# Attention feeding a gated MLP: scores and values head by head, without zero blocks, from the third batch on

## The chip, the cores and the metric

One core of one Trainium2 chip. The time is device microseconds of one execution, the median of three runs. A core has five engines that run side by side: TensorE (PE, matrix products, weights loaded by a queue of its own shown as PEld), VectorE (DVE), ScalarE (ACT), GpSimd (POOL) and SyncE (SP, which here issues every DMA). Each works through its own instructions in order and waits on semaphores for the others.

## The reference

Eight batches of eight heads, 576 queries of 64 dimensions. Keys and values are averaged over groups of 8 positions, so there are 72 of each. The attention result, 4608 tokens of 512 numbers, goes through a gated MLP with 1536 hidden units.

```python
k_p = k.reshape(B, H, Sp, pool, D).mean(axis=3)
v_p = v.reshape(B, H, Sp, pool, D).mean(axis=3)
scores = scale * np.matmul(q, k_p.transpose(0, 1, 3, 2))
attn = np.exp(scores - np.max(scores, axis=-1, keepdims=True))
attn = attn / (np.sum(attn, axis=-1, keepdims=True) + 1e-09)
x = np.matmul(attn, v_p)            # then tokens x (8 heads * 64)
g = x @ w_gate
out = (g / (1 + np.exp(-g)) * (x @ w_val)) @ w_out
```

## The kernel before

Tokens are cut into nine tiles of 512. A tile passes through the MLP in 12 steps of 128 hidden units (`moe`): 24 gate and value matmuls (`side`, lines 591 to 593, every product as high x high, low x high and high x low in 16-bit numbers), then tanh and products on ACT and DVE, then 12 projection matmuls of the step before (`project`, lines 616 to 621). Batches have 576 queries, so tile borders fall inside batches; each tile's attention is done in chunks of at most 128 queries of one batch (`_plan`). From the third batch on there are 24 chunks of 128 queries and 6 of 64.

`x` is what the MLP reads: 512 features on 4 blocks of 128 rows, tokens along the columns, a high part `xh` and a low part `xl`.

The first two batches go through `first_tile`, which interleaves attention, weight loading and the first tile's MLP by the table ORDER: a letter names a job, a number its step. There Lw loads weights, a to n split them; Ls, Lx, Ku, Vr load and sum k and v of the third batch. Everything after it is two generators: the MLP of tile i yields 12 times, and after each step three steps of the attention of tile i+1 are taken (`take(att, 3)`); a scheduler then sets the order on each engine from these by its own time model.

The attention of a chunk from the third batch on (`chunk`): q is scaled and split in a high and a low part (`split_q`, ACT and POOL). `scores` takes two heads at once: the stationary side is q of two heads on 128 rows, the moving side is 144 columns, the 72 keys of each head with zeros in the other head's 64 rows (`kst_h`, `kst_l`); three matmuls for each of four pairs. Softmax follows on DVE and ACT. `soft_high` and `soft_low` write high and low parts of the 72 weights into `half`, 64 positions of each head in 8 blocks and the remaining 8 positions of four heads in 2 more; one DMA transpose on SP turns these 10 blocks (`turned`, line 473) into `pt`. `values` then has V stationary, two heads in one 128x128 block with zeros off the diagonal, and `pt` moving, four matmuls for each of four pairs; the result has features on rows, and ACT and DVE write it straight into `xh` and `xl` (lines 490 and 494).

`prep` prepares a batch: k and v are loaded in pieces into a pool of three buffers (`mid`, which also holds q for its maximum, and the output on its way out), summed on POOL (`pool8`), the largest q, k and v are found on DVE, summed over rows by a matmul with ones (`over_rows`, line 155), and powers of two from these scale the splits.

## Time and profile before

| what | number |
|---|---|
| median of 3 runs | 1008.49 us (1005.98 to 1009.74) |
| profiled execution | 1008.23 us, span 1005.7 us |
| PE busy | 941.1 us, 94% of the span |
| DVE, ACT, POOL busy | 568.0, 411.3, 259.6 us |
| mean granted PE clock | 0.992 |
| DMA | 79.49 MB, 40 transposes of `half`, each 10 blocks |

The span runs from the first to the last instruction of the core, and the time of an execution is 2.5 us longer. Busy times of PE are modelled at their end and overlap, so the distance between the starts of two matmuls tells what one costs in a full PE.

### The profile page before, as it was taken

Reading aid. Unit: us, or ns where it says so; the run is one execution under the profiler, and the core shown is the slowest. Engines: PE = TensorE matmul, PEld = TensorE weight load, DVE = VectorE, ACT = ScalarE, POOL = GpSimd, SP = SyncE. Lnnn points to the kernel's source line nnn. Section 1 sums busy time; section 2 is a strip of 40 time slices with the busy share of each in tenths; the row PEclk is TensorE's granted clock in tenths of the full one; section 3 lists DMA queues with packets and bytes.
Section 4 is the critical chain, followed back from the end, with each engine's and each line's share of the span. In section 5 each row is a group of like instructions: output and inputs, shape, how many; then the busy total and the mean of one; then the engine's idle time right before and its main releaser. Section 6 shows DMA issues by size and latency. Waiting matters only on the chain.

```text
span 1005.7 us, 13356 instructions
## 1 busy us (share of the span) xinstructions
PE 941.1 (94%) x5200; PEld 498.2 (50%) x5200; DVE 568.0 (56%) x1047; ACT 411.3 (41%) x716; POOL 259.6 (26%) x286
## 2 busy tenths in 40 slices
PE   1478888999999999999999999999999999999997
PEld 1366443454545555555455554555455455544443
DVE  9988998467556645664357544735454245323222
ACT  4488886225323432352235423522444244322222
POOL 6656567342106210620061105200111011000000
PEclk9989999999999999999999999999999999999999
DMA  9565752432115200620061206200311011001001
GB/s 353 110 197 159 209 190 77 157 120 43 37 55 173 55 18 32 202 51 6 31 198 42 31 1 217 59 14 6 79 26 33 1 56 27 14 1 42 1 1 42
DMA packets 82942, 79.49 MB, mean 79 GB/s; under 512 B 53696, under 2 KB 70080, under 8 KB 81344
## 3 DMA queue, kind: packets, MB, share of 16 engines
q1 hardware_dynamic: 82880, 78.66, 27.0%
q8 instruction: 40, 0.66, 0.3%
q14 instruction: 22, 0.18, 0.1%
HBM read 57.41 MB, written 9.44 MB: 66 GB/s over the span
## 4 chain that ended last, share of the span: by engine, by line
PE 79%; DVE 14%; DMA 3%; ACT 2%; issue 1%; POOL 1%; SPq 0%; DVEq 0%; ACTq 0%; POOLq 0%
PE gv L591 16%; PE gv L592 16%; PE gv L593 16%; PE acc L616 9%; PE acc L620 8%; PE acc L621 8%; DVE wf L198 2%; DVE wgv_l L230 2%; DVE ws L178 1%; ACT ws L188 1%; PE ps L417 1%; DVE ws L186 1%; DMA k<-k_rows 1%; DVE sm L440 1%; DVE sc L429 1%
## 5 line engine op out<-in xcount | busy, mean ns | idle before, releaser
L591 PE MATMUL gv<-xh,wgv_h 128*128 128x512 f16 (+1 forms) x888 | 331.8, 374 | 12.0 <-DVE hf L602 9.5
L593 PE MATMUL gv<-xh,wgv_l 128*128 128x512 f16 (+1 forms) x888 | 332.0, 374 | 5.3 <-DVE wgv_l L230 5.3
L592 PE MATMUL gv<-xl,wgv_h 128*128 128x512 f16 (+1 forms) x888 | 331.9, 374 | 0.6 <-DVE xl L494 0.6
L602 DVE SCALAR_TENSOR_TENSOR hf<-hf,gv 128x512 f32<-128x512 f32 (+1 forms) x111 | 74.4, 670 | 191.7 <-ACT hf L599 191.6
L620 PE MATMUL acc<-hl,wo_b 128*128 128x512 bf16 (+1 forms) x444 | 167.4, 379 | 1.3 <-POOL hl L744 1.3
L621 PE MATMUL acc<-hb,wo_l 128*128 128x512 bf16 (+1 forms) x444 | 166.5, 377 | 0.0
L616 PE MATMUL acc<-hh,wo_h 128*128 128x512 f32 (+1 forms) x444 | 141.4, 437 | 0.0
L599 ACT ACTIVATE hf<-gv,un 128x512 f32<-128x512 f32 (+1 forms) x111 | 74.8, 674 | 162.5 <-PE gv L593 158.8
L640 ACT CAST hh<-hf 128x512 fp32r<-128x512 f32 x96 | 59.2, 617 | 198.6 <-DVE hf L607 198.4
L593 PEld LDWEIGHTS <-wgv_l 128*128 128x128 f16 x888 | 87.0, 98 | 106.4 <-DVE wgv_l L230 7.8
L592 PEld LDWEIGHTS <-wgv_h 128*128 128x128 f16 x888 | 86.9, 98 | 102.7 <-issue 13.6
L591 PEld LDWEIGHTS <-wgv_h 128*128 128x128 f16 x888 | 88.0, 99 | 91.4 <-ACT wgv_h L225 1.0
L607 DVE SCALAR_TENSOR_TENSOR hf<-gv,un,hf 128x512 f32<-128x512 f32 (+1 forms) x111 | 81.4, 733 | 80.8 <-PE gv L593 79.9
L399 POOL TENSOR_TENSOR ql<-qt,qh 128x512 f16<-128x512 f32 (+1 forms) x30 | 31.9, 1063 | 366.4 <-PE ps L419 231.5
L642 DVE TENSOR_TENSOR hl<-hf,hh 128x512 bf16<-128x512 f32 x96 | 71.8, 748 | 52.2 <-ACT hh L640 52.1
L616 PEld LDWEIGHTS acc<-hh,wo_h 128*128 128x128 f32 x444 | 82.2, 190 | 23.6
L468 POOL TENSOR_TENSOR half<-sc,half 128x512 f16<-128x512 f32 (+1 forms) x40 | 48.4, 1211 | 138.9 <-issue 81.2
L620 PEld LDWEIGHTS <-wo_b 128*128 128x128 bf16 x444 | 43.5, 98 | 65.7 <-issue 28.5
L621 PEld LDWEIGHTS <-wo_l 128*128 128x128 bf16 x444 | 44.1, 99 | 39.4 <-issue 2.2
L641 ACT CAST hb<-hf 128x512 bf16<-128x512 f32 x96 | 58.9, 613 | 0.0
L397 ACT ACTIVATE qt<-qt,inv 128x512 f32<-128x512 f32 (+1 forms) x30 | 20.1, 677 | 66.7 <-DMA qt<-q_rows 58.3
L428 DVE TENSOR_REDUCE mx<-ps 128x4 f32<-128x288 f32 (+1 forms) x80 | 35.7, 449 | 18.4 <-PE ps L419 18.2
(109 smaller groups left out, 1114.9 us busy)
## 6 DMA issues: line engine op xcount, KB each, us to landing
ws<-w_all SPq DMA_DIRECT2D x12, 1536.0 KB, 7.2
out_t<-ob SPq DMA_DIRECT2D x36, 256.0 KB, 2.3
qt<-q_rows SPq DMA_DIRECT2D x32, 256.0 KB, 3.3
vr<-v_main SPq DMA_DIRECT2D x16, 512.0 KB, 5.5
kr<-k_rows SPq DMA_DIRECT2D x14, 576.0 KB, 4.8
qr<-q_rows SPq DMA_DIRECT2D x12, 576.0 KB, 4.9
vr<-v_left SPq DMA_DIRECT2D x8, 512.0 KB, 4.3
k<-k_rows SPq DMA_DIRECT2D x2, 576.0 KB, 8.5
```

Source lines behind the costliest of these rows:

```text
L591: nc.tensor.matmul(o, wh, x["h"][:, j, a:e], start=(j == 0), stop=False)
L592: nc.tensor.matmul(o, wh, x["l"][:, j, a:e], start=False, stop=False)
L593: nc.tensor.matmul(o, wl, x["h"][:, j, a:e], start=False, stop=(j == NJ - 1))
L599: nc.scalar.activation(hf, gate, AF.Tanh, scale=un[:, c, 0:1])
L602: nc.vector.scalar_tensor_tensor(out=hf, in0=hf, scalar=1.0, in1=gate, op0=ALU.add, op1=ALU.mult)
L607: nc.vector.scalar_tensor_tensor(out=hf, in0=val, scalar=un[:, c, 2:3], in1=hf, op0=ALU.mult, op1=ALU.mult)
L616: nc.tensor.matmul(o, wo_h[:, c, js], hh[:, :n], start=begin, stop=False)
L620: nc.tensor.matmul(o, wo_b[:, c, js], hl[:, :n], start=False, stop=False)
L621: nc.tensor.matmul(o, wo_l[:, c, js], hb[:, :n], start=False, stop=end)
L640: nc.scalar.copy(hh[:, :n], hf[:, :n])
L641: nc.scalar.copy(hb[:, :n], hf[:, :n])
L642: nc.vector.tensor_sub(hl[:, :n], hf[:, :n], hh[:, :n].bitcast(F32))
```

## The change

For batches 2 to 7 attention no longer works on two heads at once. A chunk's q comes twice, once on rows 0 to 63 and once on rows 64 to 127, from an array that holds it so (`q_twice`, 8 heads side by side, twice the bytes); `split_q` writes the high part into the upper half of the rows on ACT, and high and then low into the lower half (ACT, DVE). A score product of one head is then two matmuls of 72 columns: against `ka`, the keys' high part on both halves, and `kb`, the low part above zeros.

Softmax weights are laid out as 16 blocks, two a head: 64 high and 64 low, and a block with the 72 high ones, 8 low ones and 8 high ones of the remainder (104 rows). They are turned by one DMA transpose and are now the stationary side; the moving side is 64 columns of `va` or `vb`. The result has queries on rows. ACT and DVE write its high and low part into `xt`, and a second DMA transpose of 8 blocks writes them into `x`, now one tile with both parts.

k and v of a batch come in four pieces each, k with its rows twice, v as 104 rows. All operands of two chunks live in `box`, which takes the two buffers of the weight loads once these are done. The loads and sums of the third batch leave ORDER and are made by the generator during the second tile, as for the other batches. In the generator a chunk's softmax now comes ahead of the values of the chunk before, and two steps more are left ahead of the last values of a tile.

```diff
--- before.py
+++ after.py
+VROWS = 104
...
-d10 P8 w11 d11 x11 V12 e10 y11 T8 Z6 t12 l11 u12 Lx0 n11 f10 e11 O11 g10 m11 v12 h10
+V12 e10 y11 T8 Z6 t12 l11 u12 n11 f10 e11 O11 g10 m11 v12 h10 un10 x12 i10 n10 l10 f11
...
-    halves = [const.tile([P, (2 * NJ + 2) * P], F16, name=f"half{i}") for i in range(2)]
+    halves = [const.tile([P, 2 * H * P], F16, name=f"half{i}") for i in range(2)]
...
+    home = {}
+    turn = [0]
+
+    def box(b):
+
+        if not home:
+            for i in range(2):
+                whole = raw.tile([P, 12 * P * 2], F32, name="box", tag="raw")
+                at16, part = whole.bitcast(F16), {}
+                lo = 0
+                for name, n in (("ka", SP), ("kb", SP), ("va", D), ("vb", D), ("qs", P), ("xt", P)):
+                    part[name] = at16[:, lo : lo + H * n].rearrange("p (h n) -> p h n", h=H)
+                    lo += H * n
+                home[i] = part
+                n = (SP, D)[i]
+                home[("ks", "vs")[i]] = whole[:, lo // 2 : lo // 2 + H * n].rearrange(
+                    "p (h n) -> p h n", h=H
+                )
+                nc.gpsimd.memset(part["kb"][D:], 0.0)
+                nc.gpsimd.memset(halves[i][:, OLD:], 0.0)
+        return home[b % 2]
...
     def prep_k(b):
-        for g in range(2):
-            if ("k", b, g) not in state:
-                k_load(b, g)
-                k_sum(b, g)
-                yield
+        box(b)
+        for g in range(H // 2):
+            hs = slice(2 * g, 2 * g + 2)
+            kr = mid.tile([P, 2, S], F32, name="kr", tag="mid")
+            nc.sync.dma_start(out=kr, in_=k2[b - SPLIT, :, hs])
+            pool8(nc.gpsimd, kr, home["ks"][:, hs], SP)
+            yield
...
+        hi, lo = box(b)["ka"], box(b)["kb"][:D]
+        nc.vector.tensor_scalar_mul(hi, home["ks"], inv[:, b, 1:2])
+        nc.vector.scalar_tensor_tensor(
+            out=lo, in0=home["ks"][:D], scalar=inv[:D, b, 1:2], in1=hi[:D],
+            op0=ALU.mult, op1=ALU.subtract,
+        )
...
+    def split_v(b):
+        va, vb, vs = box(b)["va"], box(b)["vb"], home["vs"]
+        sv = inv[:, b, 2:3]
+        nc.vector.tensor_scalar_mul(va[:D], vs[:D], sv[:D])
+        nc.sync.dma_start(out=va[D:], in_=va[:D])
+        nc.vector.scalar_tensor_tensor(
+            out=vb[:D], in0=vs[:D], scalar=sv[:D], in1=va[:D], op0=ALU.mult, op1=ALU.subtract
+        )
+        nc.vector.tensor_scalar_mul(vb[D:VROWS], vs[D:VROWS], sv[D:VROWS])
+        end = slice(96, VROWS)
+        nc.vector.scalar_tensor_tensor(
+            out=vb[end], in0=vs[end], scalar=sv[end], in1=vb[end], op0=ALU.mult, op1=ALU.subtract
+        )
...
+            qts = []
+            for g in range(2 if b >= SPLIT else 1):
+                qt = qp.tile([P, NJ, P], F32, name="qt")
+                src = q2[b - SPLIT, :, g * GH : (g + 1) * GH] if b >= SPLIT else q[b]
+                nc.sync.dma_start(out=qt[:, :, :n], in_=src[:, :, s0 : s0 + n])
+                qts.append(qt)
...
-        qt = load_q(b, s0, n)[:, :, :n]
-        qh = at.tile([P, NJ, P], F16, name="qh")
-        ql = at.tile([P, NJ, P], F16, name="ql")
-        nc.scalar.activation(qt, qt, AF.Copy, scale=inv[:, b, 0:1])
-        nc.scalar.copy(qh[:, :, :n], qt)
-        nc.gpsimd.tensor_sub(ql[:, :, :n], qt, qh[:, :, :n])
-        return qh, ql
+        qs = box(turn[0])["qs"]
+        for g in range(2):
+            hs = slice(g * GH, (g + 1) * GH)
+            qt = load_q(b, s0, n)[g][:, :, :n]
+            o, sq = qs[:, hs, :n], inv[:, b, 0:1]
+            nc.scalar.activation(o, qt, AF.Copy, scale=sq)
+            nc.vector.scalar_tensor_tensor(
+                out=o[D:], in0=qt[D:], scalar=sq[D:], in1=o[D:], op0=ALU.mult, op1=ALU.subtract
+            )
+        return qs
...
-                qh, ql = split
-                o = pss[j // 2][:n, 2 * SP * (j % 2) : 2 * SP * (j % 2 + 1)]
-                kh, kl = (t[i][:, j].rearrange("p g s -> p (g s)") for t in (kst_h, kst_l))
-                nc.tensor.matmul(o, qh[:, j, :n], kh, start=True, stop=False)
-                nc.tensor.matmul(o, qh[:, j, :n], kl, start=False, stop=False)
-                nc.tensor.matmul(o, ql[:, j, :n], kh, start=False, stop=True)
+                    nc.tensor.matmul(o, qt[rows, j, :n], ksum[b][rows, j], start=True, stop=True)
+        else:
+            for h in range(H):
+                o = pss[h // GH][:n, (h % GH) * SP : (h % GH + 1) * SP]
+                qs, ka, kb = split[:, h, :n], box(b)["ka"][:, h], box(b)["kb"][:, h]
+                nc.tensor.matmul(o, qs, ka, start=True, stop=False)
+                nc.tensor.matmul(o, qs, kb, start=False, stop=True)
...
+    def soft_blocks(n, sc, half):
+        a = half[:n, : H * P].rearrange("p (h d s) -> p h d s", h=H, d=2)
+        z = half[:n, H * P :].rearrange("p (h c) -> p h c", h=H)
+        most, rest = sc[:n, :, :KMAIN], sc[:n, :, KMAIN:]
+        nc.scalar.copy(a[:, :, 0], most)
+        nc.scalar.copy(z[:, :, :SP], sc[:n])
+        nc.scalar.copy(z[:, :, 96:VROWS], rest)
+        nc.gpsimd.tensor_sub(a[:, :, 1], most, a[:, :, 0])
+        nc.gpsimd.tensor_sub(z[:, :, SP : SP + KLEFT], rest, z[:, :, KMAIN:SP])
...
+    def values_of_heads(b, n, pt):
+        ps = bank()[:n]
+        va, vb = box(b)["va"], box(b)["vb"]
+        for h in range(H):
+            o = ps[:, h * D : (h + 1) * D]
+            nc.tensor.matmul(o, pt[:, h, :n], va[:, h], start=True, stop=False)
+            nc.tensor.matmul(o, pt[:VROWS, H + h, :n], vb[:VROWS, h], start=False, stop=True)
+        return ps
+
+    def x_turned(ps, n, x, off, ratio, xt):
+
+        xt = xt.rearrange("p h n -> p (h n)")[:n]
+        hi, lo = xt[:, :DM], xt[:, DM:]
+        nc.scalar.activation(hi, ps, AF.Copy, scale=ratio[:n])
+        nc.vector.scalar_tensor_tensor(
+            out=lo, in0=ps, scalar=ratio[:n], in1=hi, op0=ALU.mult, op1=ALU.subtract
+        )
+        nc.sync.dma_start_transpose(out=x["all"][:, :, off : off + n], in_=xt)
...
+            next(g)
+            if t + 1 < len(gens):
+                next(gens[t + 1])
+            yield
             if before is not None:
...
+        for _ in range(3):
+            yield
...
-        return {
-            "h": xp.tile([P, NJ, TILE], F16, name="xh"),
-            "l": xp.tile([P, NJ, TILE], F16, name="xl"),
-            "mt": small.tile([P, 3], F32, name="mt"),
-        }
+        x = xp.tile([P, 2 * NJ, TILE], F16, name="x")
+        mt = small.tile([P, 3], F32, name="mt")
+        return {"all": x, "h": x[:, :NJ], "l": x[:, NJ:], "mt": mt}
...
-            "Ls": lambda g: k_load(2, g), "Lx": lambda g: v_load(2, g),
-            "Ku": lambda g: k_sum(2, g), "Vr": lambda g: v_sum(2, g),
...
-        nc.gpsimd.memset(kst_h[i], 0.0)
-        nc.gpsimd.memset(kst_l[i], 0.0)
...
+    def twice(a):
+        a = a[SPLIT:].transpose(0, 3, 1, 2)
+        return np.concatenate([a, a], axis=1)
+
+    k6 = k.reshape(B, H, sp, POOLW, D).swapaxes(2, 3).reshape(B, H, S, D)
+    v7 = v.reshape(B, H, sp, POOLW * D)[SPLIT:].transpose(0, 2, 1, 3)
+    v_rows = np.zeros((B - SPLIT, VROWS, H, POOLW * D), np.float32)
+    v_rows[:, :KMAIN] = v7[:, :KMAIN]
+    for lo in (64, 72, 96):
+        v_rows[:, lo : lo + KLEFT] = v7[:, KMAIN:]
```

The program's order on the engines shows three places. The first is POOL near the end of the first tile; L468 and L469 write the low softmax parts, L252 to L254 (after: L255 to L257) are sums of loaded k or v, L744 (after: L833) is a low part of the MLP. Before:

```order
L469 TENSOR_TENSOR half_127<-sc,half_127 128x2x32
L449 TENSOR_TENSOR sc<-sc,ri 64x576
L252 TENSOR_TENSOR vr<-vr 128x2x256
L253 TENSOR_TENSOR vr<-vr 128x2x128
L254 TENSOR_TENSOR vs<-vr 128x128
L252 TENSOR_TENSOR kr<-kr 128x2x288
L253 TENSOR_TENSOR kr<-kr 128x2x144
L254 TENSOR_TENSOR ksum_112<-kr 128x144
L468 TENSOR_TENSOR half_126<-sc,half_126 64x512
L469 TENSOR_TENSOR half_126<-sc,half_126 64x2x32
L744 TENSOR_TENSOR hl<-hf,hh 128x512
```

After, at the same place:

```order
L522 TENSOR_TENSOR half_123<-sc,half_123 128x2x32
L502 TENSOR_TENSOR sc<-sc,ri 64x576
L521 TENSOR_TENSOR half_122<-sc,half_122 64x512
L522 TENSOR_TENSOR half_122<-sc,half_122 64x2x32
L294 MEMSET box 64x576
L833 TENSOR_TENSOR hl<-hf,hh 128x512
```

One v and one k sum are gone from between the softmax parts, and a memset of `box` stands ahead of the MLP's low part.

The second place is SP at the end of the first tile, where its output is stored. Before, with the third batch's k and v loaded around it (behind the stores, q is the third batch's and k the fourth's):

```order
L309 DMA vr<-v_main 128x1024
L266 DMA kr<-k_rows 128x1152
L309 DMA vr<-v_main 128x1024
L657 DMA out_t<-ob 128x512 x4
L289 DMA qr<-q_rows 128x1152 x2
L266 DMA kr<-k_rows 128x1152 x2
```

After:

```order
L538 DMA_TRANSPOSE pt<-half_122 128x10x64
L748 DMA out_t<-ob 128x512 x4
L303 DMA kr<-k_twice 128x1152 x4
L411 DMA vr<-v_rows 104x1024 x4
L316 DMA qr<-q_rows 128x1152 x2
```

All eight loads of the third batch's k and v now stand behind the four stores, and its q behind them.

The third place is SP at the end of the second tile, with the last chunks of the next tile's x. Before:

```order
L384 DMA qt<-q_rows 128x4x128
L473 DMA_TRANSPOSE pt<-half_127 128x10x128
L384 DMA qt<-q_rows 128x4x128
L473 DMA_TRANSPOSE pt<-half_126 128x10x128
L657 DMA out_t<-ob 128x512 x4
```

After:

```order
L538 DMA_TRANSPOSE pt<-half_123 128x16x128
L434 DMA qt<-q_twice 128x4x128
L538 DMA_TRANSPOSE pt<-half_122 128x16x128
L571 DMA_TRANSPOSE x<-box 128x8x128 x2
L748 DMA out_t<-ob 128x512 x4
```

Two transposes into `x` come last before the stores; the next tile's MLP reads what they write.

More of the change, by code (lines that the diff above doesn't have):

```diff
@@ L136, in attention_then_swiglu @@
     ksum = [const.tile([P, NJ, SP], F32, name=f"ksum{i}") for i in range(2)]
-    kst_h = [const.tile([P, NJ, 2, SP], F16, name=f"kst_h{i}") for i in range(2)]
-    kst_l = [const.tile([P, NJ, 2, SP], F16, name=f"kst_l{i}") for i in range(2)]
     p2s = const.tile([P, B, 4], F32, name="p2s")
@@ L292, in size_q @@
         nc.vector.tensor_max(mx[:, 0:1], mx[:, 0:1], mx[:, 2:3])
-        largest(mx[:, 1:2], ksum[b % 2])
+        largest(mx[:, 1:2], home["ks"])
     def split_k(b):
-        for g in range(2):
-            rows = slice(g * D, (g + 1) * D)
-            src, hi, lo = ksum[b % 2][rows], kst_h[b % 2][rows, :, g], kst_l[b % 2][rows, :, g]
-            sk = inv[rows, b, 1:2]
-            nc.vector.tensor_scalar_mul(hi, src, sk)
-            nc.vector.scalar_tensor_tensor(
-                out=lo, in0=src, scalar=sk, in1=hi, op0=ALU.mult, op1=ALU.subtract
-            )
-    def v_load(b, g):
-        home = (xp, ("xh", "xl")[g]) if b == 0 and g < 2 else (mid, "mid")
-        vr = home[0].tile([P, 2, POOLW * D], F32, name="vr", tag=home[1])
+        hi, lo = box(b)["ka"], box(b)["kb"][:D]
[17 more added lines that the diff above has]
+        )
+    def v_load(b, g):
+        if b == 0 and g < 2:
+            if "v0" not in state:
+                state["v0"] = xp.tile([P, 4, POOLW * D], F32, name="v0", tag="x")
+            vr = state["v0"][:, 2 * g : 2 * g + 2]
+        else:
+            vr = mid.tile([P, 2, POOLW * D], F32, name="vr", tag="mid")
         nc.sync.dma_start(out=vr, in_=vm[b, :, 2 * g : 2 * g + 2] if g < 2 else vl[b])
@@ L360, in prep_v @@
     def prep_v(b):
-        for g in range(3):
-            if ("v", b, g) not in state:
-                v_load(b, g)
-                v_sum(b, g)
-                yield
+        for g in range(H // 2):
+            hs = slice(2 * g, 2 * g + 2)
+            vr = mid.tile([P, 2, POOLW * D], F32, name="vr", tag="mid")
+            nc.sync.dma_start(out=vr[:VROWS], in_=v2[b - SPLIT, :, hs])
+            pool8(nc.gpsimd, vr[:VROWS], home["vs"][:VROWS, hs], D)
+            yield
         mx, _ = sizes(b)
         yield from size_q(b, mx)
-        v_largest(b)
-        v_total(b)
-        v_scale(b)
+        nc.gpsimd.memset(mx[96:, 2:3], 0.0)
+        largest(mx[:VROWS, 2:3], home["vs"][:VROWS])
+        pow2_above(p2s[:, b, :3], inv[:, b], over_rows(mx[:, :3]))
         nc.vector.tensor_scalar(
@@ L382, in load_q @@
         if (b, s0) not in queries:
-            qt = qp.tile([P, NJ, P], F32, name="qt")
-            nc.sync.dma_start(out=qt[:, :, :n], in_=q[b, :, :, s0 : s0 + n])
-            queries[b, s0] = qt
+            qts = []
[4 more added lines that the diff above has]
+                qts.append(qt)
+            queries[b, s0] = qts
         return queries[b, s0]
@@ L469, in soft_low, with turned @@
         nc.gpsimd.tensor_sub(left[:, 2], over, left[:, 0])
-    def turned(n, half):
-        pt = at.tile([P, 2 * NJ + 2, P], F16, name="pt")
-        nc.sync.dma_start_transpose(out=pt[:, :, :n], in_=half[:n])
+    def soft_blocks(n, sc, half):
[7 more added lines that the diff above has]
+        nc.gpsimd.tensor_sub(z[:, :, SP : SP + KLEFT], rest, z[:, :, KMAIN:SP])
+    def turned(n, half, blocks):
+        pt = at.tile([P, 2 * H, P], F16, name="pt")
+        nc.sync.dma_start_transpose(out=pt[:, :blocks, :n], in_=half[:n, : blocks * P])
         return pt
@@ L520, in chunk @@
             split = split_q(b, s0, m) if b >= SPLIT else None
+            me = turn[0]
+            turn[0] += 1
+            half = halves[me % 2]
             yield
@@ L534, in chunk @@
                 ratios.update(scales(bs, x["mt"]))
-            psv = values(b, m, pt)
-            x_high(psv, m, x, off, ratios[b])
-            x_low(psv, m, x, off, ratios[b])
+            if split is None:
+                psv = values(b, m, pt)
+                x_high(psv, m, x, off, ratios[b])
+                x_low(psv, m, x, off, ratios[b])
+            else:
+                x_turned(values_of_heads(b, m, pt), m, x, off, ratios[b], box(me)["xt"])
             yield
@@ L552, in attention @@
             yield
-            if before is not None:
-                next(before)
-                yield
             next(g)
@@ L559, in attention @@
             yield
+            if before is not None:
+                next(before)
+                yield
             before = g
-        yield
+        for _ in range(3):
+            yield
         next(before)
```

63 lines of the change are left out of this document (33 added, 30 removed).

## The prediction, made before the run

> **What bounds the kernel now.** I read the page first, then busy time by stretches, then what TensorE (PE) waited for, and last PE's instructions one by one.
>
> ```profile
> span 1005.7 us, 13356 instructions
> PE 941.1 (94%) x5200; PEld 498.2 (50%) x5200; DVE 568.0 (56%) x1047; ACT 411.3 (41%) x716; POOL 259.6 (26%) x286
> PE 79%; DVE 14%; DMA 3%; ACT 2%; issue 1%; POOL 1%; SPq 0%; DVEq 0%; ACTq 0%; POOLq 0%
> ...
> 125.00:150.00 25.00, 21.25 (x127) 10.99 (x126) 24.47 (x34) 20.28 (x30) 15.82 (x12) 0.93 0.51 184
> 150.00:175.00 25.00, 21.14 (x104) 10.16 (x103) 22.18 (x33) 16.17 (x30) 17.55 (x17) 0.93 0.29 76
> ...
> 400.00:500.00 100.00, 100.00 (x545) 51.95 (x543) 52.88 (x104) 37.05 (x67) 23.93 (x27) 1.00 0.25 72
> ...
> PE gv L591 <- DVE hf L602: 5.0, 4, 2.5
> PE ps L155 <- DVE xl L494: 2.4, 1, 2.4
> ```
>
> The first three rows are the page: PE is busy for 94% and the chain that ended last is 79% PE and 14% VectorE (DVE). The window rows (length, then PE, PEld, DVE, ACT, POOL busy, granted clock, DMA) show two regimes. Up to 175 us, the hand-ordered first tile, DVE is full (24.47 of 25 us) and PE has gaps. From then on PE is full at clock 1.00 and DVE half idle. The last rows are PE's own waits from 150 us to the end: the longest two. So a nanosecond of PE time removed after 175 us is a nanosecond of span, unless a wait takes its place; the attention of batches 2 to 7 lies there.
>
> **PE's share of the change.** A busy time of a matmul contains its pipeline, so its cost in a full PE is the distance from start to start.
>
> ```profile
> 323.92 0.22 PE L483 MATMUL ps<-pt,vst_h 128*128 128x128 f16 x1
> 323.97 0.22 PE L484 MATMUL ps<-pt,vst_h 128*128 128x128 f16 x1
> ...
> 324.83 0.23 PE L417 MATMUL ps<-kst_h,qh 128*128 128x144 f16 x1
> ...
> 325.20 0.38 PE L591 MATMUL gv<-xh,wgv_h 128*128 128x512 f16 x1
> ...
> 365.22 0.19 PE L483 MATMUL ps<-pt,vst_h 128*128 128x64 f16 x1
> ...
> 365.70 0.38 PE L591 MATMUL gv<-xh,wgv_h 128*128 128x512 f16 x1
> ```
>
> Sixteen value matmuls of 128 columns run from 323.92 to 324.83: 57 ns each. The six score matmuls of 144 columns after them end at 325.20: 62 ns each. Sixteen value matmuls of 64 columns (a chunk of 64 queries) run from 365.22 to 365.70: 30 ns each, each with its own 128x128 weights. That last row is the very shape of the new value matmul: other weights every time, 64 columns moving. The new score matmul moves 72; between 64 columns at 30 ns and 144 at 62 ns it costs 30 to 62, in proportion 33 ns, and I take that.
>
> Before, a chunk has 4 x 3 score and 4 x 4 value matmuls; after, 8 x 2 and 8 x 2. For 128 queries: 12 x 62 + 16 x 57 = 1.66 us before, 16 x 33 + 16 x 30 = 1.01 us after: 0.65 us less. For 64 queries the values already cost 30 ns: 12 x 62 + 16 x 30 = 1.22 before, 1.01 after, 0.21 less. These short chunks pay something else:
>
> ```profile
> 315.37 0.38 PE L621 MATMUL acc<-hb,wo_l 128*128 128x512 bf16 x1
> 315.68 0.25 PE L419 MATMUL ps<-kst_h,ql 128*64 128x144 f16 x1
> ...
> 315.89 0.23 PE L419 MATMUL ps<-kst_h,ql 128*64 128x144 f16 x1
> 316.05 0.39 PE L591 MATMUL gv<-xh,wgv_h 128*128 128x512 f16 x1
> ...
> L417 PE MATMUL ps<-kst_h,qh 128*128 128x144 f16 x96 | 20.3, 227 | 0.3 <-DVE sc L429 0.3
> L417 PE MATMUL ps<-kst_h,qh 128*64 128x144 f16 x24 | 5.3, 238 | 0.0
> ```
>
> Going from 128-column weights to 64-column weights and back costs about 0.1 us each way: 0.31 us from L621 to L419 where two neighbouring L621/L620 are 0.22 apart, and 0.16 us from L419 to L591 where 0.06 is usual. After the change the values of a short chunk have 64-column weights too (the stationary side is now the transposed softmax), so one more pair of edges, 0.2 us: a short chunk gains nothing. The counts are in the last two rows, groups by line and shape, four matmuls a chunk: 24 full and 6 short chunks. PE: 24 x 0.65 = 15.7 us less. The bounds, if 72 columns cost 62 ns or 30: 24 x (0.65 - 0.46) = 4.5 us and 16.8 us.
>
> The Trainium skill's page "TensorE: Matmul & The Clock Gate", section "Back-to-back issue gap", speaks against this: with hardware decode off the sequencer needs about 62 ns for any matmul, however short. By it the time would be rival 3's. The rows from 365.22 disagree, at 30 ns.
>
> **The first tile.** Loads and sums of the third batch (Lx, Ls, Ku, Vr) leave the hand-written order. They are POOL and DMA work, but POOL slows DVE, which sets the pace there:
>
> ```profile
> 127.91 0.95 DVE L178 TENSOR_SCALAR ws<-ws 128x1536 uint32<-128x1536 uint32 x1
> 147.07 2.49 DVE L178 TENSOR_SCALAR ws<-ws 128x1536 uint32<-128x1536 uint32 x1
> 139.98 0.14 DVE L220 TENSOR_TENSOR p2w<-p2w 128x1 f32<-128x1 f32 x1
> 152.23 1.21 DVE L220 TENSOR_TENSOR p2w<-p2w 128x1 f32<-128x1 f32 x1
> ...
> 147.46 1.28 POOL L252 TENSOR_TENSOR vr<-vr 128x512 f32<-128x512 f32 x1
> 152.01 1.41 POOL L252 TENSOR_TENSOR kr<-kr 128x576 f32<-128x576 f32 x1
> 162.34 0.35 PE L155 MATMUL ps<-wm,ones 128*128 128x2 f32 x2 [2.38 <-DVE xl L494]
> ```
>
> The same DVE instructions take 1.5 and 1.1 us longer while POOL adds (Vr2 at 147.46, Ku1 at 152.01), and PE later waits 2.38 us for DVE. Without these sums that is up to 2.6 us. POOL's other work moves forward and may meet DVE elsewhere, so it is 0 to 5 us (the upper end: the wait at 162.34 and the half-speed clock after it, 0.07 of the 50 us in the 0.93 rows, gone with it); I take 2.5 us less.
>
> **What comes back as waits.** The moved preparation starts behind the first tile's stores on SP, since its tiles share a pool of three buffers with them.
>
> ```profile
> 186.85 3.09 SPq L657 DMA_DIRECT2D out_t<-ob  x4
> kr<-k_rows SPq DMA_DIRECT2D x14, 576.0 KB, 4.8
> ...
> 176.21 1.41 POOL L252 TENSOR_TENSOR kr<-kr 128x576 f32<-128x576 f32 x1
> 181.18 0.46 POOL L254 TENSOR_TENSOR vs<-vr 128x128 f32<-128x128 f32 x1
> ...
> 197.40 1.29 PE L616 MATMUL acc<-hh,wo_h 128*128 128x512 f32 x4
> ...
> 200.26 0.38 PE L591 MATMUL gv<-xh,wgv_h 128*128 128x512 f16 x1
> ```
>
> One k and one v sum together run from 176.21 to 181.64: 2.7 us each. Stores end at 190 and the first k lands 4.8 us later, at 195; eight sums are 21.6 us, to 216.6. Then an addition for the next batch (1.4) stands on POOL ahead of the small memset that the value maximum needs, and DVE takes that maximum (0.7 by L494 below): near 219 to 221. In the new PE order the sum of these maxima over rows stands behind the projection that ends at 200.26, two stretches of 24 gate/value and 12 projection matmuls (5.2 and 2.9 us each) and one of 24 and 6: 200.3 + 16.2 + 6.6, near 223. A margin of 2 us: I count 0.5 us, between 0 and 8.
>
> The x of every chunk now passes a second DMA transpose. In the new order the last values of tiles 2 and 3 stand 9 gate/value and 16 projection matmuls, and 20 projection matmuls, ahead of the first matmul that reads that x: some 5 us.
>
> ```profile
> pt<-half SPq DMA_TRANSPOSE x40, 3.4
> ...
> L490 ACT ACTIVATE xh<-ps,r 128x512 f16<-128x512 f32 x32 | 21.8, 683 | 19.4 <-PE ps L486 19.4
> L494 DVE SCALAR_TENSOR_TENSOR xl<-ps,r,xh 128x512 f16<-128x512 f32 x32 | 23.7, 742 | 12.4 <-ACT xh L490 12.4
> ...
> 328.92 1.24 SPq L473 DMA_TRANSPOSE pt<-half  x1
> 333.49 0.19 PE L483 MATMUL ps<-pt,vst_h 128*128 128x64 f16 x1
> ```
>
> Chain: matmuls 0.7, ScalarE 0.68 and DVE 0.74 with some queue, transpose 2.7 to 3.4 (8 blocks, by the row for 10): 5.5 to 6 us. At those two places I expect 1 us each, 0 to 4. The later tiles have 12 us or more there. The softmax transpose goes from 10 to 16 blocks: 3.4 us at least, 5.4 in proportion. A ScalarE copy grows from 64 to 576 columns, at most 0.7 us by L490's 0.68 for 512, so the values get their input up to 2.7 us later. The closest cover before is 333.49 - 328.92 - 3.4 = 1.2 us, and the new order puts values 1.6 to 1.9 gate/value stretches behind their scores instead of about 1.4: hidden but for about 0.5 us in all.
>
> DVE gains the lower half of the queries, two instructions a chunk. Nearest is L494 at 0.74 us for the same width: 24 x 1.5 + 6 x 1 = 42 us, less some 8 us of cheaper preparation; POOL loses the low part of q and gains two k sums and one v sum a batch, 8 us by the 2.7 above. With 568 us busy of 1006 DVE has room, and POOL more. But more DVE work means more of the 5.0 us that PE waits for hf: I add 1 us, 0 to 6. The wider ScalarE copies and the doubled q and k loads lie on engines 41% busy and, for DMA, at 0.25 in the stretch from 400 us; they cost nothing until those fill. On SP the copy of half of va waits for DVE once a batch, and the next loads of k and q stand behind it; they are ahead of their use by several us, so nothing again. The memsets of the new blocks run once, on POOL.
>
> Sum: 1005.7 - 15.7 - 2.5 + 0.5 + 2 + 0.5 + 1 = 991.5 us span. The profiled execution took 1008.23, 2.5 us around its span, and the median is 1008.49: 994.0 us. A difference under 0.5% (5 us) would not be told from none.
>
> **Rivals.**
> (1) The covers fail where they are thinnest: preparation 8 us late, both tile ends 4 us, DVE 6 us. Half of these 22 us instead of the 3.5 counted gives 1001.5, all of them 1012.5. For it: margins of 2 us and below, worked out from durations on a less crowded POOL. Against: PE meets the old order's tight places too, and its two longest sums of waits from 150 us on are 5.0 and 2.4 us.
> (2) Slower: the transposed softmax arrives late at every chunk, since PE takes its instructions in order and gate/value work stands behind the values. It decides from 15.7 / 30 = 0.52 us a chunk. If the full 2.7 us came against the closest cover of 1.2, every chunk would lose 1.5 us, 45 us in all: 1039. Against: the later places of the values, and a DMA busy for a quarter.
> (3) Slower by another way: a pair of weight load and matmul has a floor near 60 ns. Then 32 x 0.062 = 1.98 us a chunk against 1.66 and 1.22: 24 x 0.32 + 6 x 0.76 = 12 us more instead of 15.7 less: 1022. The row at 365.22 speaks against it, save that its weights were loaded from resident tiles and the new ones come fresh from a transpose. This floor would be the 62 ns of the Trainium skill's page named above.
> (4) The matmul gain comes with none of the 4 us of waits, and the first tile gains 5 us instead of 2.5: 987.5.
>
> **How the numbers follow.** Forecast 994 (988 to 1000): 0.66. Rival 4, below 988: 0.10. Rival 1, 1000 to 1008: 0.16, of which half is within 0.5% of 1008.5 (from 1003.4). Rivals 2 and 3: 0.05 and 0.03. So faster 0.84, same 0.08, slower 0.08. Range 986 to 1003: it leaves out the slower rivals, the tail of (1) and a little of (4).
>
> **What would show it.** Right: new value matmuls 30 ns and score matmuls 33 ns from start to start; no PE matmul waiting for a transpose by more than 2 us; L178 in the first tile near 1 us at each place; PE still full from 200 us on, and the next tiles each some 2 us shorter. Wrong: PE waits named for pt or x at many chunks, a long wait of the sum over rows near 220 us, starts 60 ns apart, or a granted clock under 1.00 after 200 us.

## The result and the profile after

The changed kernel takes 1020.38 us (median of 4 runs, 1018.55 to 1022.95) against 1008.73 us for the kernel before beside it: ratio 1.0122, 95% interval 1.0091 to 1.0153. Slower by 1.2%, where 994 was forecast. The page of the profile after, in the order of the rows shown before (span, busy engines, the chain that ended last):

```profile
span 1017.6 us, 13953 instructions
PE 931.9 (92%) x5320; PEld 483.6 (48%) x5320; DVE 610.5 (60%) x1059; ACT 424.6 (42%) x716; POOL 277.8 (27%) x316
PE 58%; DVE 16%; DMA 14%; POOL 5%; ACT 4%; issue 2%; SPq 0%; POOLq 0%; DVEq 0%; ACTq 0%
```

PE is busy 9 us less, as a cheaper attention should make it, but the span is 12 us longer, and the chain is now 58% PE instead of 79%: DVE, DMA and POOL have taken the rest. Windows of the kernel after (length, then PE, PEld, DVE, ACT, POOL busy, granted clock, DMA) say where:

```profile
150.00:175.00 25.00, 23.13 (x120) 11.40 (x118) 19.68 (x34) 16.37 (x30) 11.25 (x11) 1.00 0.09 8
...
400.00:500.00 100.00, 89.39 (x516) 44.65 (x514) 61.17 (x102) 35.24 (x61) 35.37 (x42) 1.00 0.49 124
500.00:600.00 100.00, 96.39 (x566) 48.39 (x565) 66.45 (x117) 39.68 (x70) 30.18 (x36) 0.98 0.51 126
600.00:700.00 100.00, 96.06 (x537) 47.91 (x537) 56.96 (x104) 37.55 (x65) 27.11 (x33) 0.97 0.47 117
700.00:800.00 100.00, 100.00 (x592) 50.83 (x591) 58.02 (x116) 41.03 (x72) 7.10 (x10) 1.00 0.31 64
```

The end of the first tile is better than before (23.13 of 25 us busy at full clock, where it was 21.14 at 0.93). From 400 to 500 us, where PE was full before, it is busy 89.39; then it also runs at a clock of 0.98 and 0.97. From 700 us on, where no batch is left to prepare (the last split ends at 705), it is full again. PE's own waits of the kernel after, from 150 us to the end (engine, tile and line, what it waited for: us in all, times, longest):

```profile
PE gv L682 <- DVE hf L693: 12.7, 10, 3.6
PE gv L682 <- DVE hf L698: 7.5, 4, 3.1
PE ps L559 <- DMA pt<-half: 3.8, 4, 2.1
PE ps L471 <- DVE sc L482: 2.8, 2, 1.5
PE ps L158 <- DVE mx L308: 1.5, 1, 1.5
```

The largest is the MLP's own gate product: its PSUM bank isn't free because DVE hasn't yet read it (L693 and L698 are the tanh product and the value product of `moe`). DVE isn't full there, at 61.17 of 100 us. What it does instead is in its waits from 180 to 760 us, first after, then before:

```profile
DVE mx L308 <- DMA qr<-q_rows: 38.9, 11, 6.9
DVE mx L308 <- POOL box L257: 13.5, 6, 3.9
DVE mx L308 <- POOL mx L416: 2.5, 3, 2.0
```

```profile
DVE mx L281 <- DMA qr<-q_rows: 15.3, 9, 4.2
DVE mx L281 <- POOL ksum L254: 10.9, 4, 3.7
```

It stands at the maxima of the next batch's q, k and v (L308, L281 before) for 54.9 us instead of 26.2, because their data is not there. DVE takes its instructions in order, so the MLP's product behind the maximum waits too. One such place in the timeline of the kernel after (start, duration, engine and line; in brackets the idle time before it and what ended it):

```profile
395.72 3.44 SPq L748 DMA_DIRECT2D out_t<-ob  x4
399.25 2.08 SPq L411 DMA_DIRECT2D vr<-v_rows  x3
411.43 1.45 SPq L316 DMA_DIRECT2D qr<-q_rows  x2
...
404.84 1.27 POOL L255 TENSOR_TENSOR vr<-vr 104x512 f32<-104x512 f32 x1 [20.31 <-DMA vr<-v_rows]
412.04 0.86 POOL L257 TENSOR_TENSOR box<-vr 104x128 f32<-104x128 f32 x2
...
415.12 1.35 DVE L308 TENSOR_REDUCE mx<-qr 128x1 f32<-128x1152 f32 x1 [5.94 <-DMA qr<-q_rows]
418.88 1.35 DVE L308 TENSOR_REDUCE mx<-qr 128x1 f32<-128x1152 f32 x1 [2.40 <-DMA qr<-q_rows]
420.15 0.68 DVE L693 SCALAR_TENSOR_TENSOR hf<-hf,gv 128x512 f32<-128x512 f32 x1
...
420.88 0.38 PE L682 MATMUL gv<-x,wgv_h 128*128 128x512 f16 x1 [3.63 <-DVE hf L693]
```

Behind four output stores, which use the same three buffers, three v pieces take them from 399.25 on; their sums on POOL start at 404.84 and the last ends at 412.9; q's loads go out at 411.43, when buffers come free; DVE stands 5.94 and 2.40 us for them; the product of the MLP behind them starts at 420.15, and PE has waited 3.63 us for it. At this place of the kernel before DVE stood 3.18 us, and PE did not wait:

```profile
422.76 1.35 DVE L281 TENSOR_REDUCE mx<-qr 128x1 f32<-128x1152 f32 x1 [3.18 <-DMA qr<-q_rows]
```

### The profile page after: what moved, and what is told of

The parts are those of the page before. It is cut to its first block, busy times and chain, and to the rows that moved or that the text cites. A ratio compares the mean times of both kernels' runs of the same rounds, so it can differ in the third digit from the quotient of the medians.

```text
span 1017.6 us, 13953 instructions
## 1 busy us (share of the span) xinstructions
PE 931.9 (92%) x5320; PEld 483.6 (48%) x5320; DVE 610.5 (60%) x1059; ACT 424.6 (42%) x716; POOL 277.8 (27%) x316
## 4 chain that ended last, share of the span: by engine, by line
PE 58%; DVE 16%; DMA 14%; POOL 5%; ACT 4%; issue 2%; SPq 0%; POOLq 0%; DVEq 0%; ACTq 0%
PE gv L682 12%; PE gv L684 12%; PE gv L683 12%; PE acc L707 7%; PE acc L711 6%; PE acc L712 6%; DMA vr<-v_rows 5%; DMA qr<-q_rows 2%; DMA out_t<-ob 2%; DMA pt<-half 2%; POOL vr L255 2%; DVE wgv_l L233 2%; DMA kr<-k_twice 1%; POOL box L257 1%; DVE wf L201 1%
## 5 line engine op out<-in xcount | busy, mean ns | idle before, releaser
L682 PE MATMUL gv<-x,wgv_h 128*128 128x512 f16 (+1 forms) x888 | 334.0, 376 | 27.1 <-DVE hf L693 17.2
L684 PE MATMUL gv<-x,wgv_l 128*128 128x512 f16 (+1 forms) x888 | 334.3, 376 | 5.5 <-DVE wgv_l L233 5.5
L683 PE MATMUL gv<-x,wgv_h 128*128 128x512 f16 (+1 forms) x888 | 334.0, 376 | 0.6 <-DVE x L578 0.6
L693 DVE SCALAR_TENSOR_TENSOR hf<-hf,gv 128x512 f32<-128x512 f32 (+1 forms) x111 | 74.3, 669 | 176.9 <-ACT hf L690 176.5
L533 POOL TENSOR_TENSOR half<-sc,half 128x512 f16<-128x512 f32 (+1 forms) x30 | 34.7, 1156 | 312.0 <-issue 260.0
L698 DVE SCALAR_TENSOR_TENSOR hf<-gv,un,hf 128x512 f32<-128x512 f32 (+1 forms) x111 | 81.3, 732 | 62.5 <-PE gv L684 60.7
L711 PEld LDWEIGHTS <-wo_b 128*128 128x128 bf16 x444 | 43.6, 98 | 65.3 <-issue 28.1
L255 POOL TENSOR_TENSOR kr<-kr 128x576 f32<-128x576 f32 x26 | 39.3, 1512 | 107.3 <-DMA kr<-k_twice 106.8
L255 POOL TENSOR_TENSOR vr<-vr 104x512 f32<-104x512 f32 (+1 forms) x28 | 36.3, 1298 | 65.9 <-DMA vr<-v_rows 65.1
L451 ACT ACTIVATE box<-qt,inv 128x512 f16<-128x512 f32 (+1 forms) x60 | 39.3, 672 | 33.2 <-PE ps L472 20.2
```

What stands on the lines that cost most here:

```text
L255: eng.tensor_add(a, a, b4)
L682: nc.tensor.matmul(o, wh, x["h"][:, j, a:e], start=(j == 0), stop=False)
L683: nc.tensor.matmul(o, wh, x["l"][:, j, a:e], start=False, stop=False)
L684: nc.tensor.matmul(o, wl, x["h"][:, j, a:e], start=False, stop=(j == NJ - 1))
L693: nc.vector.scalar_tensor_tensor(out=hf, in0=hf, scalar=1.0, in1=gate, op0=ALU.add, op1=ALU.mult)
L698: nc.vector.scalar_tensor_tensor(out=hf, in0=val, scalar=un[:, c, 2:3], in1=hf, op0=ALU.mult, op1=ALU.mult)
```

## The experiments

Batches are counted from one in the expectations: the third is the first of the changed form, 4 to 8 are those prepared later. All times are medians, ratios are to the kernel before on the same chip. "PE waits" are the sums of PE's waits from 200 us on, "standing" those of DVE at the maxima, 200 to 760 us, both from the profiled run.

| run | us | ratio [95%] | PE waits | standing |
|---|---|---|---|---|
| before | 1008.7 | 1 | 4.3 | 25.6 |
| after | 1020.4 | 1.0122 [1.0091, 1.0153] | 28.1 | 54.9 |
| e1_after_no_prep | 985.4 | 0.9754 [0.9728, 0.9780] | 2.2 | 10.9 |
| e2_before_no_prep | 1001.4 | 0.9917 [0.9889, 0.9945] | 0.0 | 0.0 |
| e12_loads_only | 985.6 | 0.9765 [0.9751, 0.9780] | 3.8 | 10.5 |
| e9_loads_and_sums | 999.6 | 0.9903 [0.9883, 0.9923] | 14.3 | 12.1 |
| e15_maxima_of_resident | 1004.7 | 0.9960 [0.9947, 0.9974] | 17.7 | 9.7 |
| e14_k_once | 1007.2 | 0.9993 [0.9977, 1.0008] | 18.4 | 27.7 |
| e17_tied | 1006.5 | 0.9976 [0.9963, 0.9990] | 17.1 | 13.8 |
| e18_k_max_last | 1008.8 | 1.0000 [0.9986, 1.0013] | 19.2 | 25.5 |
| e13_q_own_place | 1023.3 | 1.0144 [1.0125, 1.0164] | 27.7 | 65.5 |
| e16_both | 1014.9 | 1.0061 [1.0046, 1.0077] | 23.0 | 36.4 |

The span follows PE's waits more nearly than the standing: from e1 to after, 25.9 us more waits and 34.4 us more span (983.2 to 1017.6). The rest is mostly the clock, granted below 1.00 in three of the 100 us windows after 300 us, some 7 us.

**Is it the preparation?** Preparation of batches 4 to 8 left out, of after and of before (there with 8 steps instead of 11):

```diff
     def prep(b):
+            if b > SPLIT:
+                for _ in range(11):
+                    yield
+                return
```

> The changed kernel, but batches 4 to 8 are not prepared: no loads, sums, maxima or splits of their k, v and q maxima; they use the third batch's operands and scales (so their results are not the reference's). Theory A (preparation): the changed kernel loses some 22 us of PE waits and 7 us of half clock because DVE, in order, stands at the maxima of a later batch until its loads and sums arrive; without them PE waits less than 8 us after 150 us and the time is 988 to 994. Theory B (transposes): the two transposes of every chunk make PE wait for pt and x by themselves; then it stays above 1005.

> The kernel before with the same left out (batches 4 to 8 use the third batch's operands and scales). Theory A: its preparation is nearly hidden already, so only its 5 to 8 us of waits can go: 1001 to 1007, and e1 is faster than this by 10 to 15 us, the matmul gain. Theory B: e1 is not faster than this.

985.43 and 1001.38 us, the first even below theory A's range. Without the preparation the change gains 16.0 us. With it, preparing these five batches costs 35.0 us after and 7.4 before. So the loss is there, and all that the change does to attention itself is a gain.

**One part of it?** The q loads and maxima for scales:

```diff
         for g in range(2):
+            if b == SPLIT:
                 qr = mid.tile([P, NJ // 2, S], F32, name="qr", tag="mid")
                 ...
+        else:
+            nc.vector.tensor_copy(out=mx[:, 0:1], in_=qmax)
```

> The changed kernel, where only the loads of q for its maximum, and those maxima, are left out for batches 4 to 8 (the third batch's maximum is used). Theory A with q's maxima as the place (DVE stood 39 us for these loads): 994 to 1004. Theory A with the sums of k and v as the place: above 1010. Theory B: above 1012.

1012.8 us, ratio 1.0033 [1.0015, 1.0051]: q's maxima are not the place by themselves. The number is what theory A with the sums had, and theory B's bound of 1012 doesn't exclude it. Where DVE stands moves on; its waits from 180 to 760 us in this run:

```profile
DVE mx L309 <- POOL box L257: 48.8, 11, 8.0
```

**The second transpose?** x written directly in the shape that the MLP reads, with no transpose (its values are then not the transposed ones; POOL zeroes what a chunk of 64 queries leaves unwritten):

```diff
-        nc.scalar.activation(hi, ps, AF.Copy, scale=ratio[:n])
+        nc.scalar.activation(hi, src, AF.Copy, scale=ratio[:n])
...
-        nc.sync.dma_start_transpose(out=x["all"][:, :, off : off + n], in_=xt)
```

> The changed kernel without the second transpose: ACT and DVE write x directly, so what the MLP reads is not turned. Theory B (30 transposes of 8 blocks slow the DMA or come late): below 1006. Theory A: the waits stay at the maxima, 1012 to 1021.

1018.54 us, ratio 1.0086 [1.0054, 1.0118]: 1.8 us less than after, which is not clear of the two intervals, and far from the 1006 of theory B. For the second transpose that theory falls.

**A backlog of one batch?** The fourth and the eighth batch unprepared, each in turn:

```diff
+            if b == 3:      # e6: b == 7
+                for _ in range(1):
+                    yield
+                return
```

> The changed kernel, with only the fourth batch left unprepared (it uses the third's operands and scales, so its results are not the reference's). Theory A1 (backlog): since the third batch's loads and sums left ORDER and a preparation has 11 steps instead of 8, the generator is one preparation behind, so that a batch is prepared in the very tile in which its scores are due, right behind the output's stores; with one preparation taken out the sums over rows stand at the end of the tile before, as in the kernel before, and nearly all of the 35 us go: 988 to 1000. Theory A2 (each preparation costs its own wait): one of five, 7 us: 1010 to 1015.

> The same, but the eighth batch is left unprepared instead of the fourth. Theory A1: by then the lag is worked off, so at most the fifth tile's loss goes: 1009 to 1019. Theory A2: one of five again, 1010 to 1015, the same as the run without the fourth.

1018.08 (1.0091 [1.0062, 1.0120]) and 1016.4 us (1.0071 [1.0049, 1.0092]). One preparation less gives 2 to 4 us: not the 20 us and more that a backlog would give with the fourth left out, and less than the fifth part that theory A2 had. No backlog, then, and no equal share for each preparation either. With the fourth left out the waits only changed their name, from hf to the other reader of PSUM that stands behind a maximum on DVE (L571, the low part of x):

```profile
PE ps L474 <- DVE box L571: 17.2, 4, 6.5
```

**The pace?** Four steps of attention after each MLP step instead of three, after and before:

```diff
-            take(att, 3)
+            take(att, 4)
```

> The changed kernel with nothing left out, but four steps of the next tile's attention after each step of the MLP instead of three. Theory A1: the lag is gone from the third tile on, 990 to 1002, faster than before. Theory A2: the same loads, sums and maxima as before this edit, 1012 to 1022.

> The kernel before with four steps instead of three. Theory A1: it had no lag, so within 5 us of 1008. If the pace by itself were worth something in any kernel: 1000 or less.

1027.35 (1.0185 [1.0149, 1.0221]) and 1015.68 us (1.0064 [1.0045, 1.0084]). Both lie outside every range given. Earlier is worse in both kernels, by 7 us: a shortage of steps is not what makes the work late. The longest of PE's waits in e7, now for the transposed softmax:

```profile
PE ps L559 <- DMA pt<-half: 18.5, 7, 4.9
```

**Loads, sums or VectorE work?** Preparation of batches 4 to 8 built up again: loads and sums without DVE's work, and loads alone.

```diff
             pool8(nc.gpsimd, kr, home["ks"][:, hs], SP)      # e12: only if b == SPLIT, v too
...
+            if b == SPLIT:
                 largest(mx[:, 2 * g : 2 * g + 1], qr)
+        if b > SPLIT:
+            return
```

> The kernel after with all loads and all POOL sums of the preparation of batches 4 to 8, but none of its VectorE work (maxima, scales, splits); those batches are computed with the third batch's operands, so their values are left out. Theory A (what costs is VectorE standing in its order at maxima whose data is late): the loads and sums alone cost little, 985 to 993 us, and PE's waits after 150 us stay under 8 us. Theory B (the traffic itself costs: loads ahead of the transposes in SP's queue and on the DMA engines make the softmax late for PE): 1005 us or more, with PE waiting for pt.

> As the run with loads and sums, with the POOL sums left out too: only the loads of batches 4 to 8 are issued, and nobody reads them. Theory A: 984 to 990 us. Theory B: 1000 us or more. If POOL's sums slow VectorE and PE is held by that (theory C), this run is at least 5 us faster than the one with the sums.

985.63 us with the loads alone: doubled k included, they cost 0.2 us, so theory B in its plain form falls. (Nobody reads these loads, so a buffer is free as soon as its load has landed.) The sums add 14.0 us, the VectorE work the remaining 20.8. That the sums cost so much neither theory A nor B foresaw; theory C did, with its 5 us or more. DVE is indeed slower beside the sums: the low part of the queries takes 824 ns in e9 and 698 in e12 (means from 230 to 760 us). But PE's waits for hf grow only from 3.1 to 4.2 us, and those for pt from 0.2 to 8.9; how much of the latter comes from a slower DVE is not separated. PE's largest wait in e9:

```profile
PE ps L564 <- DMA pt<-half: 8.9, 4, 4.1
```

How the longest of the four came about, in the timeline of e9:

```profile
305.26 0.24 ACT L537 CAST half<-sc 128x64 f16<-128x64 f32 x1
...
310.73 1.71 POOL L255 TENSOR_TENSOR vr<-vr 104x512 f32<-104x512 f32 x1 [2.87 <-DMA vr<-v_rows]
312.40 1.15 POOL L538 TENSOR_TENSOR half<-sc,half 128x512 f16<-128x512 f32 x1
...
313.86 1.74 SPq L303 DMA_DIRECT2D kr<-k_twice  x2
315.70 6.51 SPq L543 DMA_TRANSPOSE pt<-half  x2
...
322.94 0.20 PE L564 MATMUL ps<-box,pt 128*128 128x64 f16 x1 [4.13 <-DMA pt<-half]
```

And the same instruction of POOL in the run with loads alone:

```profile
305.32 1.17 POOL L540 TENSOR_TENSOR half<-sc,half 128x512 f16<-128x512 f32 x1 [35.04 <-issue]
```

POOL too works in order. The low part of the softmax is POOL's (`soft_blocks`), and ScalarE had its part ready at 305.50 in e9; but additions of the v sums stand ahead of it, and one of them waits 2.87 us for its load, so it starts at 312.40, 7 us late. Its transpose goes out at 315.70 behind two k loads on SP, and PE waits 4.13 us. Without sums the low part starts at once, after 35 us with nothing to do.

**SP's queue?** The loads of k, v and q issued by POOL:

```diff
-            nc.sync.dma_start(out=kr, in_=k2[b - SPLIT, :, hs])
+            nc.gpsimd.dma_start(out=kr, in_=k2[b - SPLIT, :, hs])      # vr, qr too
```

> The kernel after, complete, with the preparation's loads of k, v and q issued from POOL's queue instead of SP's, so that a load which waits for a free buffer no longer holds the transposes and loads behind it on SP. If the waiting in SP's queue makes the maxima late (theory D): VectorE's standing at the maxima falls below 25 us (from about 55) and the time is 1008 us or less. If the lateness comes from the chain of load, sum and next load through three buffers (theory A's form), the standing stays and the time is 1015 to 1022 us.

1018.3 us, ratio 1.0078 [1.0052, 1.0104]. DVE stands 33.0 us at q and 15.0 at the sums, little less than in after. SP's order is not the cause, or what it costs is paid on POOL instead, which issues now.

```profile
DVE mx L308 <- DMA qr<-q_rows: 33.0, 8, 7.8
DVE mx L308 <- POOL box L257: 15.0, 4, 5.3
```

**Maxima later by steps?**

```diff
+            yield
             yield
+            largest(mx[:, 2 * g : 2 * g + 1], qr)
```

> The kernel after, complete, with the two maxima of q taken two generator steps after their load is issued instead of in the same step, which adds two steps to each batch's preparation. Theory A: less standing of VectorE at qr, and 1003 to 1013 us, unless the scheduler's own order of the maxima doesn't follow the steps. Theory B: 1017 us or more, since the loads are as many and the steps are fewer.

1029.18 us, ratio 1.0197 [1.0180, 1.0214]. That is within theory B's 1017 or more, but not for its reason. The standing stayed, at 59.7 us: the loads of q still go out only when sums on POOL free their buffers, for which SP waits 22.3 us in this run and 20.7 in after. That the added steps delayed the whole attention of a tile is the likely reason for the loss, and not shown. New among PE's waits is the x of a tile's last chunk:

```profile
PE gv L683 <- DMA x<-box: 14.8, 5, 4.7
```

**Standing, or the work itself?** The same VectorE instructions, but with the maxima taken of resident weights:

```diff
-        largest(mx[:, 1:2], home["ks"])
+        largest(mx[:, 1:2], home["ks"] if b == SPLIT else resident(H, SP))      # q and v too
```

> The kernel after with the same VectorE instructions, but for batches 4 to 8 the maxima of q, k and v are taken of as many numbers of the resident output weights, so that nothing of theirs is waited for; the scales of those batches are therefore not the right ones. Loads, sums and splits stay. Theory A (VectorE's standing at the maxima is what the last 21 us are): 998 to 1006 us, near the run with loads and sums alone (999.6). Rival (the added VectorE work itself, maxima and splits): 1013 us or more.

1004.67 us: of the 20.8 us of VectorE work 15.7 go with the standing, and 5.1 remain for the work, its waits and its order. This is a size and not an exact split, for three reasons. The scheduler's order changes: 7.9 of e15's 17.7 us of PE's waits are one wait at 221 us, at the third batch, which the edit leaves as it was. Nobody reads the q pieces, so their buffers come free sooner and the chain of loads is shorter too. And DVE stands another 8.7 us at the split of v, which the table doesn't count. For the 14.0 us of the sums the same kind of standing, on POOL, is shown at the place above, not at all of them.

**The shared buffers, or the number of pieces?** q in a place of its own; k loaded once in two pieces and two sums as before, then copied to the per-head form; and both, with half of q.

```diff
# e13
+            nc.gpsimd.tensor_copy(out=q_piece(g)[:D, 0, :1], in_=home["vs"][:D, H - 1, :1])
+            nc.sync.dma_start(out=q_piece(g), in_=q[b, :, g * NJ // 2 : (g + 1) * NJ // 2])
# e14
+        for g in range(2):
+            kr = mid.tile([P, NJ // 2, S], F32, name="kr", tag="mid")
+            nc.sync.dma_start(out=kr, in_=k[b, :, js])
+            pool8(nc.gpsimd, kr, ksum[b % 2][:, js], SP)
+        for g in range(2):
+            for lo in (0, D):
+                nc.gpsimd.dma_start(out=ks[lo : lo + D, g], in_=ksum[b % 2][g * D : (g + 1) * D])
```

> The kernel after, complete, with q of batches 4 to 8 loaded for its maximum not through the three shared buffers but into the space of the first two batches' operands, behind the last v sum of the batch before. If the shared buffers make q late (the chain of load, sum and next load): no standing at q, and 1000 to 1010 us. If the data engines are simply slow there or VectorE's work is the cause: 1014 us or more.

> The kernel after, complete, with k loaded once, in two pieces and two sums as in the kernel before, and its sums then copied by four small transfers to the per-head form with the rows twice. If the number of loads and sums in the chain is the cause: 1004 to 1012 us. If it is not: 1016 us or more.

> The kernel after, complete, with k loaded once as in the run before this one, and the first half of q loaded into the space of the first two batches' operands. If the chain through the shared buffers is the cause, this has five loads less in it a batch... that is, 7 of 10 tiles instead of 10, as against 7 in the kernel before, and should give 995 to 1005 us, faster than both kernels. If not, 1012 us or more.

(The last one's "five loads less" is a slip: it is three, 7 instead of 10, as its own next words have it.) e14 takes 1007.2 us, 13.2 less than after, the largest single part of the loss that a complete kernel gets back. It changes two things: k comes in fewer pieces, and the k sums of two batches have a place each (`ksum`), as in the kernel before. In after there is one place for all, and POOL, in order, waits for DVE to split the batch before (from 200 to 760 us):

```profile
POOL box L257 <- DVE box L327: 10.2, 4, 2.9
```

No run tells the two apart. e13 is no faster than after (1023.3), and e16 is 7.7 us slower than e14. Getting q early does not help, because DVE then stands at the sums of k and v; e13's waits of DVE from 180 to 760 us:

```profile
DVE mx L318 <- POOL box L260: 45.4, 11, 7.0
DVE mx L318 <- DMA spare<-q_rows: 11.6, 6, 3.4
```

So the three buffers don't make it by themselves: with q taken out of them DVE stands 45.4 us at the sums instead of 13.5. Why an own place for half of q costs e16 time rather than nothing stays open. (In e13 the loads of q wait 15.3 us on SP for the small copy on POOL, with the loads of k behind them.)

**Standing alone, in a complete kernel?** e14 with k's maximum put behind q's, and with all maxima of a batch put behind a product of the MLP:

```diff
# e18
+        nc.vector.tensor_copy(out=mx[:, 1:2], in_=mx[:, 0:1])
         largest(mx[:, 1:2], home["ks"])
# e17
+        yield
+        nc.vector.tensor_copy(out=mx[:, :3], in_=state["hf"][:, :3])
+        for g, qr in enumerate(qrs):
+            largest(mx[:, 2 * g : 2 * g + 1], qr)
```

> The run with k loaded once, complete, with one small VectorE copy more that puts the maximum of k behind the maxima of q in VectorE's order, so that the scheduler can't take it as soon as it believes the copied sums there. In that run VectorE stood 14.8 us at k and 12.7 us at q. If standing is the cause: 10 to 16 us of standing in all, and 997 to 1003 us. If only the number of loads and sums counts: 1005 to 1010 us.

> The run with k loaded once, complete, with all maxima of a batch put together behind the last product of the MLP step that runs then (a small copy of three of its columns into the place of the maxima), one generator step later than before. If standing is the cause: under 15 us of standing and 996 to 1003 us, unless the batch is then ready too late and PE waits for its operands at the start of a tile, which would show as waits for the scores' bank or for box. If only the number of loads and sums counts: 1005 to 1010 us.

Both miss what standing as the cause would give, and lie where they were to be if only the number of loads and sums counts, 1005 to 1010. e18 (1008.76) only moves the standing, from k to q, and so tells nothing of its price. e17 does what it should: DVE stands 13.8 us instead of 27.7, these two rows the largest,

```profile
DVE mx L313 <- DMA qr<-q_rows: 8.4, 5, 2.7
DVE mx L313 <- POOL mx L426: 5.4, 4, 3.2
```

and yet it is 1006.5 us, 0.7 less than e14, with as much waiting of PE (17.1 against 18.4). The largest of its rows is now the transposed softmax:

```profile
PE ps L569 <- DMA pt<-half: 6.7, 2, 3.4
```

So theory A, that DVE's standing is what costs, is borne out for the kernel after (e15, with the reservations there) but not beyond it: with half of e14's standing gone, PE waits elsewhere for as long, and what makes it wait there was not tried. e17 is faster than both kernels, by 0.24% [0.10%, 0.37%] against before: the 16 us of the cheaper attention are still mostly eaten by its preparation.

## Why the prediction was wrong

**Matmuls: right.** Term: 24 chunks at 0.65 us, from 33 ns a score and 30 ns a value matmul. The first and last of 16 score matmuls and of 16 value matmuls in the kernel after:

```profile
240.57 0.20 PE L471 MATMUL ps<-box 128*128 128x72 f16 x1
...
241.06 0.20 PE L472 MATMUL ps<-box 128*128 128x72 f16 x1
...
260.87 0.19 PE L559 MATMUL ps<-box,pt 128*128 128x64 f16 x1
...
261.35 0.19 PE L560 MATMUL ps<-box,pt 104*128 104x64 f16 x1
```

15 steps in 0.49 and 0.48 us: 33 and 32 ns. Rival 3, with its 60 ns, is out. That the weights come fresh from a transpose made a difference of 2 ns at most (32, where resident ones took 30). The product is a little off, 24 x 0.65 being 15.6 and not 15.7. The Trainium skill's page "TensorE: Matmul & The Clock Gate", section "Back-to-back issue gap", gives for one matmul alone N/2.4 + 2.5 ns, which is 32.5 for 72 columns; the trace agrees with that, though these matmuls stand in a row, and not with the 62 ns of its table's note.

**First tile: right in sign, under-sized.** 2.5 us were taken of 0 to 5. The first output store went out at 182.49 us instead of 186.85: 4.4 us. (The two parts named for the upper end, 2.4 us and 0.07 of 50 us, add up to 5.9 and not 5.) The shift that took 2.49 us beside a sum on POOL:

```profile
146.53 1.24 DVE L181 TENSOR_SCALAR ws<-ws 128x1536 uint32<-128x1536 uint32 x1
```

All terms but the 1 us for DVE came to 15.2 us of gain in the prediction (15.7 + 2.5 - 0.5 - 2 - 0.5); e2 against e1, where the later preparation is left out, measures 16.0.

**Third batch's preparation and the transposes: right.** The wait of the sum over rows was put at 0.5 us, 0 to 8, and is 1.5 (L158 above). No wait for x stands among PE's waits of after, where 2 us were allowed. PE waits 3.8 us for the transposed softmax where 0.5 was written, but in e1, with the same transposes and no later preparation, it doesn't wait for them at all: those 3.8 us belong to the step below.

**The step that failed** is the paragraph on what DVE gains, and in it two sentences. "With 568 us busy of 1006 DVE has room, and POOL more" argues from busy time; and the doubled loads "cost nothing until those fill" asks whether the engines are full. None was full on average: DVE 60%, POOL 27%, DMA 0.49 from 400 to 500 us. Loads that wait for no sum were indeed free, 0.2 us (e12). But the preparation of the five later batches was priced by its durations, 1 us with a range to 6 for hf, when what it adds is mostly lateness: ten loads and eight sums a batch through three buffers instead of seven and five, ahead of other work in queues that work in order. PE's waits for hf, 5.0 us before, came to 20.2. That step cost 27.6 us (35.0 less 7.4). With it in place of the 1 us counted there, 994.0 becomes 1020.6.

The prediction did name DVE's hf as the place where more waits would come, and rival 1, "the covers fail where they are thinnest", is the mechanism in kind: late preparation and a late DVE. It gave that rival 8 us of preparation for the third batch alone, and left the other five batches at nothing; all its covers failing came to 1012.5. The working done for the third batch, with its margin of 2 us, came out within its range, and was never done for the fourth, whose v and q loads also stand behind four output stores (from 295.41 us) in the same three buffers. The trace of before showed the place: 26 us of DVE standing at L281, in the view of waits of which the prediction shows only PE's rows.

**What stays open.** How the 27.6 us divide. 13 went in e14, with the pieces of k and the one place for its sums together. The rest of e14's cost over e1, 22 us against 7.4 before, holds v's fourth piece, two maxima of wider tiles (k's and v's) and a scheduler whose order assumed the data earlier than it came; no run takes these apart.

## What to carry to other kernels

Before an engine is called idle enough for more work, read its waits as well as its busy time: work whose input comes from a chain of loads and sums can cost less by its duration than by its lateness, and it charges that to whatever stands behind it on an engine that works in order. When one batch is prepared during another's main work, do the margin for every batch and not only for the first, and count how many pieces go through the shared buffers. To see what a side job costs, take it out whole, then put its loads, its sums and its vector work back one at a time.

## What the runs showed of the hardware

A 16-block transpose of the softmax took 4.3 us from issue to landing where the 10-block one took 3.4 (medians of e1 and of before, from 200 us on). SP's issue of one, 1.35 us in the middle and 1.8 at most before, took up to 4.7 us after and 7.3 in e12, behind loads. In after, 26 us more of PE's waits came with some 7 us of lower clock, but not wait by wait: from 300 to 320 us, with one wait of 2.61 us, the granted clock was 0.92, and from 400 to 500, with the longest wait of all (3.63), it was 1.00.
